# Rows of the expert tiles turned by DMA transposes of 2-byte halves and put together on VectorE, in place of transposes on TensorE

## The chip, the cores and the metric

The kernel runs on one core of a Trainium2 chip. The time is that of one execution on the device in microseconds, as a median over several executions. Before the change it is 495.23 us (three runs, 494.86 to 496.37). A run is called fast when it is undisturbed, and slow when it is over 1.5% above the fastest of its kernel. Each changed kernel was timed on the same chip and in the same rounds as the kernel before. A ratio is the mean time of one kernel's fast runs over the mean of the other's in the same rounds (for most experiments the first, profiled run is left out), so it isn't quite the ratio of the medians that stand beside it. The interval behind a ratio is at 95%. The experiments ran on several chips, where the kernel before had medians of 494.69 to 496.69 us. So a difference between the medians of two experiments is uncertain by some 2 us, and where it matters the difference of the ratios, times 495.5 us, stands beside it. A verdict "faster" or "slower" asks for 2%.

## The reference, cut to what matters

```python
def reference(q, k, v, lam, w_gate, w_local, w1, w2):
    x = linear_attention(q, k, v, lam)           # 4 x 768 tokens, 512 float32 each
    ... # pick one of 8 experts e[b, s] for each token (argmax of x @ w_gate, or the token before's)
    for b in range(B):
        for s in range(S):
            h = np.maximum(x[b, s] @ w1[e], 0.0)     # 512 x 1024
            out[b, s] = p[e] * (h @ w2[e])           # 1024 x 512
```

Attention comes first, then the experts. 3072 tokens are sorted by expert into tiles of 128 rows, with a few half tiles for the remainders. Everything is float32.

## The kernel before

Attention writes each token's row to a scratch tensor in DRAM. The expert part has 24 whole tiles and, with this input, three half tiles. For each tile, GpSimd gathers 128 rows with an indirect DMA. They arrive with tokens on the partitions, but the first product needs the 512 features there, so TensorE turns the tile in four 128x128 transposes and VectorE brings the result from PSUM to SBUF. SyncE issues the weight loads, 2 MB each for w1 and w2, two tiles ahead.

```python
    def rows_of(s):                                  # attention: rows to DRAM
        ...
        xn = moe.tile([P, DM], F32, name="xn")       # two buffers
        nc.scalar.copy(xn, px)
        nc.scalar.dma_start(out=x_dram[P * s:P * s + P, :], in_=xn)

    def weights(g):                                  # SyncE; skipped if the expert stays
        nc.sync.dma_start(out=w1t[g % 2], in_=w1_src(e), cond=other, cond_hint=False)
        nc.sync.dma_start(out=w2t[g % 2], in_=w2_src(e), cond=other, cond_hint=False)

    def ahead(g):                                    # gather, two tiles ahead
        collect(xgt[g % 2], *at(g))

    def turned(g):
        pt = pg.tile([P, DT, P], F32, name="po1")
        for d in range(DT):                          # DT = 4
            nc.tensor.transpose(pt[:, d], xgt[g % 2][:, P * d:P * d + P], ident)
        nc.vector.tensor_copy(xtt[g % 2], pt)

    # the stretch in which half tiles run between whole ones (three of eight steps)
            for g in range(GA, GB):
                ahead(g + 2)
                if g + 1 in half_in:
                    xh[half_in[g + 1]] = ahead_half(half_in[g + 1])
                hidden(g, 0)                         # first product
                if h is not None:
                    hs = hidden_of_half(xh.pop(h))
                hidden(g, 1)
                ...
                turned(g + 1)
                if g + 1 in half_in:
                    xh[half_in[g + 1]] = turned_half(xh[half_in[g + 1]])
                output(g)                            # second product
                ...
                weights(g + 2)
                if h is not None:
                    output_of_half(h, ht)
                    if h + 1 < n:
                        weights_of_half(h + 1)       # 4 MB more, for one half tile
```

## Time and profile before

| what | before |
|---|---|
| time, median | 495.23 us |
| TensorE busy | 475.2 us, 96% of the span |
| DMA share, 171 to 297 us (half tiles among the whole ones) | 1.01 |
| DMA share, 361 to 484 us | 0.50 |
| one whole tile late in the kernel | 14.45 us |

In all views PE is TensorE, PEld its weight loads, DVE VectorE, ACT ScalarE, POOL GpSimd and SP SyncE; L185 is a line of the kernel, and `out<-in` names the tiles written and read. The DMA share is the mean busy share of the 16 DMA engines.

Two things are read before anything else. Which engine is busy all the time? And what is second? The busy row of the page, its slices and the windows answer both, and the prediction shows them.

### The profile page before, as it was taken

How to read it: one execution, taken by the hardware profiler on the slowest of the kernel's cores; microseconds unless marked ns; L12 is line 12 of the kernel's file. 1: busy time of each engine (PE TensorE's matmuls, PEld its weight loads, DVE VectorE, ACT ScalarE, POOL GpSimd, SP SyncE). 2: the span in 40 equal slices, each digit the busy share in tenths (PEclk: the TensorE clock that was granted, in tenths of full speed). 3: DMA queues.
4: the chain of work that ended last, by engine and by line, in shares of the span. 5: the costliest groups of instructions: out<-in, count | busy, mean ns of one | idle time of the engine just before them, and what ended most of it. 6: DMA issues, size and time to landing. Idle time of an engine off the chain costs nothing. (4 is left out here: it accounts for less than half of the span.)

```text
span 493.0 us, 10193 instructions
## 1 busy us (share of the span) xinstructions
PE 475.2 (96%) x4231; PEld 351.6 (71%) x4231; DVE 127.3 (26%) x315; ACT 84.7 (17%) x212; POOL 106.8 (22%) x118
## 2 busy tenths in 40 slices
PE   6999999989999999999999999999999999999992
PEld 5877788776777667658657856876667777666770
DVE  6645677652367301011010101101110110110000
ACT  2256656331110000000000001000000000000000
POOL 5575564300101300221011100201101101110000
PEclk9899999999999999999999999999999999999997
DMA  7999999996788999999999997699954980894000
GB/s 272 411 418 380 352 342 330 401 368 233 260 319 292 324 378 399 395 376 397 398 333 386 398 398 277 211 330 319 327 194 157 310 314 31 284 332 169 23 25 17
DMA packets 49850, 146.42 MB, mean 297 GB/s; under 512 B 3244, under 2 KB 3244, under 8 KB 46960
## 3 DMA queue, kind: packets, MB, share of 16 engines
q1 hardware_dynamic: 42096, 125.86, 69.9%
q0 software_dynamic: 4224, 13.37, 7.1%
q10 hardware_dynamic: 3456, 6.29, 3.4%
q8 instruction: 36, 0.59, 0.5%
q14 instruction: 38, 0.31, 0.2%
HBM read 153.90 MB, written 12.98 MB: 338 GB/s over the span
## 5 line engine op out<-in xcount | busy, mean ns | idle before, releaser
L646 PEld LDWEIGHTS ps<-xt,w 128*128 128x128 f32 x1536 | 175.0, 192 | 14.0 <-issue 12.9
L646 PE MATMUL ps<-xt,w 128*128 128x128 f32 x1536 | 177.1, 276 | 0.8 <-DVE xt L631 0.8
L653 PE MATMUL pk<-w,ht 128*128 128x512 f32 x384 | 168.8, 592 | 0.0
L653 PEld LDWEIGHTS pk<-w,ht 128*128 128x128 f32 x384 | 71.1, 190 | 80.4 <-issue 80.4
L648 ACT ACTIVATE ht<-ps 128x512 f32<-128x512 f32 x48 | 28.7, 598 | 314.7 <-PE ps L646 314.2
L659 POOL DMA_INDIRECT out_dram<-y,sidx x24 | 24.6, 1026 | 196.3 <-DVE y L658 179.3
L658 DVE TENSOR_SCALAR y<-pk,gate 128x512 f32<-128x512 f32 x24 | 18.0, 751 | 146.0 <-PE pk L653 140.6
L637 DVE COPY xt<-po 128x512 f32<-128x512 f32 x23 | 15.9, 691 | 143.2 <-PE po L636 143.1
L621 POOL DMA_INDIRECT xg<-x_dram,gidx x24 | 25.0, 1041 | 121.2 <-PE po L636 84.1
L189 DVE TENSOR_TENSOR sm<-ps,mask 128x512 f32<-128x512 f32 x46 | 29.6, 685 | 15.1 <-PE ps L185 15.0
L165 POOL TENSOR_TENSOR qd<-inp,lamq 128x512 f32<-128x512 f32 x20 | 25.6, 1282 | 23.3 <-PE po L212 8.8
L185 PE MATMUL ps<-inp 64*64 64x128 f32 x736 | 26.3, 282 | 2.0 <-DMA inp<-in_qkv_dram 2.0
L225 PE MATMUL po<-sm,inp 128*64 128x128 f32 x384 | 26.9, 284 | 0.3 <-DMA inp<-in_qkv_dram 0.3
L225 PEld LDWEIGHTS po<-sm,inp 128*64 128x64 f32 x384 | 21.1, 140 | 7.5 <-issue 6.6
L168 POOL TENSOR_TENSOR kd<-inp,rev 128x512 f32<-128x512 f32 x20 | 22.4, 1122 | 16.1 <-PE pk L234 7.6
L185 PEld LDWEIGHTS ps<-inp 64*64 64x64 f32 x736 | 20.6, 136 | 5.6 <-issue 4.6
L246 ACT COPY xn<-pk 128x512 f32<-128x512 f32 x24 | 14.1, 588 | 30.6 <-DMA x_dram<-xn 19.8
L216 ACT ACTIVATE kv<-kv,lamq 128x64 f32<-128x64 f32 x64 | 17.1, 337 | 9.8 <-PE po L212 6.4
L228 ACT COPY xc<-po 128x256 f32<-128x256 f32 x48 | 15.3, 371 | 14.2 <-PE po L225 14.0
L244 PE MATMUL pk<-ident,xc 128*128 128x128 f32 x96 | 15.7, 286 | 0.0
L234 PE MATMUL pk<-inp,kd 128*64 128x64 f32 x320 | 13.2, 222 | 1.2 <-issue 1.1
L636 PE MATMUL po<-ident,xg 128*128 128x128 f32 x92 | 13.8, 273 | 0.0
(182 smaller groups left out, 223.6 us busy)
## 6 DMA issues: line engine op xcount, KB each, us to landing
w<-in_w_dram SPq DMA_DIRECT2D x57, 2048.0 KB
inp<-in_qkv_dram SPq DMA_DIRECT2D x22, 1024.0 KB
x_dram<-xn ACTq DMA_DIRECT2D x24, 256.0 KB
inp<-in_qkv_dram SPq DMA_DIRECT2D x4, 512.0 KB
w<-in_w_dram SPq DMA_DIRECT2D x4, 512.0 KB
xg<-x_dram,gidx POOLq DMA_INDIRECT x24, 7.0
out_dram<-y,sidx POOLq DMA_INDIRECT x24, 6.9
xgh<-x_dram,gidx POOLq DMA_INDIRECT x3, 6.4
```

The lines of the kernel that those rows point to most:

```text
L165: nc.gpsimd.tensor_tensor(qd, x[:, 0].rearrange("p (a i) -> p a i", i=P), lamq, ALU.mult)
L168: nc.gpsimd.tensor_tensor(kd.rearrange("p (h d) -> p h d", d=DH), x[:, 2].rearrange("p (h d) -> p h d", d=DH), rev.unsqueeze(2).broadcast_ ...
L185: nc.tensor.matmul(ps[u][js, a], lhsT=kt[rows, a, js], rhs=qt[rows, a], start=True, stop=True, skip_group_check=True)
L189: nc.vector.tensor_tensor(sm[:, u], ps[u], mask[:, u], ALU.mult)
L216: nc.scalar.mul(kv[:, a], kv[:, a], lamq[:, a, P - 1:P])
L225: nc.tensor.matmul(head(a, u), lhsT=vn[:, a, u], rhs=sm[:, u, a], start=(not c and a < 2), stop=True, skip_group_check=True)
L621: nc.gpsimd.indirect_dma_start(out=xg, out_offset=None, in_=x_dram[:n, :], in_offset=bass.IndirectOffsetOnAxis(ap=gidx[i][:, j:j + 1], axi ...
L646: nc.tensor.matmul(ph[:, i], lhsT=w1t[g % 2][:, d, P * f:P * f + P], rhs=xtt[g % 2][:, d], start=(d == 0), stop=(d == DT - 1))
L648: nc.scalar.activation(hts[g][:, FT // 2 * half:FT // 2 * half + FT // 2], ph, ACT.Relu)
L653: nc.tensor.matmul(pys[g % 2], lhsT=ht[:, f], rhs=w2t[g % 2][:, f], start=(f == 0), stop=(f == FT - 1))
L658: nc.vector.tensor_scalar(y, pys[g % 2], gate[i][:, j:j + 1], None, ALU.mult)
L659: nc.gpsimd.indirect_dma_start(out=out, out_offset=bass.IndirectOffsetOnAxis(ap=sidx[i][:, j:j + 1], axis=0), in_=y, in_offset=None, bound ...
```

## The change

The intent is to take the transposes off TensorE, which is the bound, and give them to the DMA engines. The DMA transpose is used here on 2-byte elements: a float32 row is stored as 512 low halves followed by 512 high halves. The tile of 128 x 1024 halves is transposed by DMA, SBUF to SBUF, and VectorE puts low and high halves together again. There is one hop more per tile, so there is a third row buffer, gathers start one tile earlier, and the transpose is issued by SyncE, in the queue of the weights. In attention, the row copy on ScalarE now splits the halves, and has four buffers in place of two.

```diff
+        xn = moe.tile([P, 2 * DM], U16, name="xn", bufs=4)
+        nc.scalar.copy(xn.rearrange("p (l f) -> p l f", l=2), px.bitcast(U16).rearrange("p (f l) -> p l f", l=2))
...
+    xgt = [moe.tile([P, 2 * DM], U16, name=f"xg{i}", bufs=1) for i in range(3)]
+    xct = [moe.tile([P, 2, DT, P], U16, name=f"xc{i}", bufs=1) for i in range(2)]
...
+    def cross(xc, xg):
+        nc.sync.dma_start_transpose(out=xc.rearrange("p l d i -> p (l d) i"), in_=xg)
...
     def turned(g):
-        pt = pg.tile([P, DT, P], F32, name="po1")
-        for d in range(DT):
-            nc.tensor.transpose(pt[:, d], xgt[g % 2][:, P * d:P * d + P], ident)
-        nc.vector.tensor_copy(xtt[g % 2], pt)
+        nc.vector.tensor_copy(xtt[g % 2].rearrange("p d i -> p (d i)").bitcast(U16).rearrange("p (k l) -> p l k", l=2),
+                              xct[g % 2].rearrange("p l d i -> p l (d i)"))
...
             for g in range(GA, GB):
                 h = half_in.get(g)
-                ahead(g + 2)
                 if g + 1 in half_in:
-                    xh[half_in[g + 1]] = ahead_half(half_in[g + 1])
+                    if half_in[g + 1] not in xh:
+                        xh[half_in[g + 1]] = ahead_half(half_in[g + 1])
+                    xh[half_in[g + 1]] = crossed_half(xh[half_in[g + 1]])
+                crossed(g + 2)
+                ahead(g + 3)
+                if g + 2 in half_in:
+                    xh[half_in[g + 2]] = ahead_half(half_in[g + 2])
                 hidden(g, 0)
... (the half tiles' copies and the other loops in the same way)
```

More of the change, by code (lines that the diff above doesn't have):

```diff
@@ L78 @@
     dram = ctx.enter_context(tc.tile_pool(name="dram", bufs=1, space=bass.MemoryType.DRAM))
-    x_dram = dram.tile([N, DM], F32, name="x_dram")
+    x_dram = dram.tile([N, 2 * DM], U16, name="x_dram")
     lt = route.tile([P, NT, E + 1], F32, name="lt")
@@ L244, in rows_of @@
             nc.tensor.transpose(px[:, P * a:P * a + P], xc[:, a, ORDER[s][0]], ident)
-        xn = moe.tile([P, DM], F32, name="xn")
-        nc.scalar.copy(xn, px)
+        xn = moe.tile([P, 2 * DM], U16, name="xn", bufs=4)
+        nc.scalar.copy(xn.rearrange("p (l f) -> p l f", l=2), px.bitcast(U16).rearrange("p (f l) -> p l f", l=2))
         nc.scalar.dma_start(out=x_dram[P * s:P * s + P, :], in_=xn)
@@ L612, in weights @@
         nc.sync.dma_start(out=w2t[g % 2], in_=w2_src(e), cond=other, cond_hint=False)
-    xgt = [moe.tile([P, DM], F32, name=f"xg{i}", bufs=1) for i in range(2)]
+    xgt = [moe.tile([P, 2 * DM], U16, name=f"xg{i}", bufs=1) for i in range(3)]
+    xct = [moe.tile([P, 2, DT, P], U16, name=f"xc{i}", bufs=1) for i in range(2)]
     xtt = [moe.tile([P, DT, P], F32, name=f"xt{i}", bufs=1) for i in range(2)]
@@ L623, in collect, with crossed, ahead_half @@
                                      bounds_check=n - 1, oob_is_err=False)
+    def cross(xc, xg):
+        nc.sync.dma_start_transpose(out=xc.rearrange("p l d i -> p (l d) i"), in_=xg)
     def ahead(g):
-        collect(xgt[g % 2], *at(g))
-    def first_turned():
-        for d in range(DT):
-            nc.tensor.transpose(pr[:, P * d:P * d + P], xgt[0][:, P * d:P * d + P], ident)
-        nc.vector.tensor_copy(xtt[0].rearrange("p d i -> p (d i)"), pr)
+        collect(xgt[g % 3], *at(g))
+    def crossed(g):
+        cross(xct[g % 2], xgt[g % 3])
+    def ahead_half(h):
+        xg = act.tile([P, 2 * DM], U16, name="xgh")
+        collect(xg, 1, GF - KA + h)
+        return xg
     def turned(g):
-        pt = pg.tile([P, DT, P], F32, name="po1")
-        for d in range(DT):
-            nc.tensor.transpose(pt[:, d], xgt[g % 2][:, P * d:P * d + P], ident)
-        nc.vector.tensor_copy(xtt[g % 2], pt)
+        nc.vector.tensor_copy(xtt[g % 2].rearrange("p d i -> p (d i)").bitcast(U16).rearrange("p (k l) -> p l k", l=2),
+                              xct[g % 2].rearrange("p l d i -> p l (d i)"))
     def hidden(g, half):
@@ L670 @@
         (18, 0): tokens_to_first_tiles, (19, 0): lambda: (brought(0, (0, 1)), masks(1)),
-        (19, 1): lambda: by_slots(0, (0, 1)), (20, 0): lambda: (ahead(0), ahead(1), rows_out(0)),
+        (19, 1): lambda: by_slots(0, (0, 1)), (20, 0): lambda: (ahead(0), ahead(1), ahead(2), rows_out(0)),
         (21, 0): lambda: chances(0), (22, 0): lambda: chances(1), (23, 0): lambda: brought(0, (2, 3, 4)),
+        (23, 1): lambda: turned(0),
     }
@@ L706 @@
                 nc.sync.dma_start(out=w2t[0], in_=w2_src(0))
-                nc.sync.dma_start(out=w1t[1], in_=w1_src(1))
-                nc.sync.dma_start(out=w2t[1], in_=w2_src(1))
-                weights(0)
-                weights(1)
             if s + 1 < NS:
@@ L721 @@
                 rows_of(s - 1)
-            if s + 1 == NS:
-                first_turned()
             if s % B == 0 and s:
@@ L726 @@
             extra_work(s, 1)
+            if s == NS - 4:
+                crossed(0)
+                crossed(1)
+                weights(0)
+                nc.sync.dma_start(out=w1t[1], in_=w1_src(1))
+                nc.sync.dma_start(out=w2t[1], in_=w2_src(1))
+                weights(1)
         x_ctx.close()
@@ L743 @@
         gates(NC - 1)
-        ahead(2)
+        crossed(2)
+        ahead(3)
         hidden(0, 1)
@@ L751 @@
         along_sequences(2)
-        ahead(3)
+        crossed(3)
+        ahead(4)
         hidden(1, 0)
@@ L762 @@
         tokens_to_other_tiles()
-        ahead(4)
+        crossed(4)
         hidden(2, 0)
@@ L776 @@
         ahead(6)
+        ahead(7)
+        first = ahead_half(0)
         rows_out(1)
@@ L779 @@
         hidden(4, 1)
+        crossed(5)
+        crossed(6)
         turned(5)
@@ L788, in weights_of_half, with crossed_half, turned_half @@
         nc.sync.dma_start(out=w2t[2], in_=w2_src(e))
-    def ahead_half(h):
-        xg = act.tile([P, DM], F32, name="xgh")
-        collect(xg, 1, GF - KA + h)
-        return xg
-    def turned_half(xg):
-        for d in range(DT):
-            nc.tensor.transpose(pr[:, P * d:P * d + P], xg[:, P * d:P * d + P], ident)
+    def crossed_half(xg):
+        xc = act.tile([P, 2, DT, P], U16, name="xch")
+        cross(xc, xg)
+        return xc
+    def turned_half(xc):
         xt = act.tile([P, DT, HP], F32, name="xth")
-        nc.vector.tensor_copy(xt, pr.rearrange("p (d i) -> p d i", i=P)[:, :, :HP])
+        nc.vector.tensor_copy(xt.rearrange("p d i -> p (d i)").bitcast(U16).rearrange("p (d i l) -> p l d i", l=2, i=HP),
+                              xc[:, :, :, :HP])
         return xt
@@ L841 @@
         weights(6)
-        first = ahead_half(0)
-        ahead(7)
+        first = crossed_half(first)
+        crossed(7)
+        ahead(8)
         hidden(5, 0)
@@ L887 @@
         for g in range(GB, GMIN - 1):
-            ahead(g + 2)
+            crossed(g + 2)
+            if g + 3 <= GMIN:
+                ahead(g + 3)
             hidden(g, 0)
@@ L898 @@
             for g in range(GMIN - 1, last):
-                if GMIN + 1 <= g + 2 < last:
-                    ahead(g + 2)
+                if GMIN < g + 2 < last:
+                    if g + 2 == GMIN + 1:
+                        ahead(g + 2)
+                    crossed(g + 2)
+                if GMIN < g + 3 < last:
+                    ahead(g + 3)
                 hidden(g, 0)
```

## The prediction

> **What bounds the kernel now.** I read the page's busy shares and slices first, then the costliest groups, then the timeline of TensorE in two places, then sums over windows, and last the queue that issues the weight loads.
>
> ```profile
> PE 475.2 (96%) x4231; PEld 351.6 (71%) x4231; DVE 127.3 (26%) x315; ACT 84.7 (17%) x212; POOL 106.8 (22%) x118
> ...
> PE   6999999989999999999999999999999999999992
> ...
> DMA  7999999996788999999999997699954980894000
> ```
>
> TensorE is busy in every slice but the first and the last; no other engine is near. But the DMA row stands at 9 in most slices up to the middle: two resources are close to full at once, and this change moves work from the first to the second.
>
> ```profile
> L646 PE MATMUL ps<-xt,w 128*128 128x128 f32 x1536 | 177.1, 276 | 0.8 <-DVE xt L631 0.8
> ...
> L637 DVE COPY xt<-po 128x512 f32<-128x512 f32 x23 | 15.9, 691 | 143.2 <-PE po L636 143.1
> ...
> L246 ACT COPY xn<-pk 128x512 f32<-128x512 f32 x24 | 14.1, 588 | 30.6 <-DMA x_dram<-xn 19.8
> ...
> L636 PE MATMUL po<-ident,xg 128*128 128x128 f32 x92 | 13.8, 273 | 0.0
> ```
>
> L636 are the transposes that go: 92, with 0.0 us of idle before them, 273 ns each by record. Records overlap, so their real price is read from starts:
>
> ```profile
> 426.64 7.31 PE L646 MATMUL ps<-xt,w 128*128 128x128 f32 x64
> 433.78 0.60 PE L636 MATMUL po<-ident,xg 128*128 128x128 f32 x4
> 434.22 7.03 PE L653 MATMUL pk<-w,ht 128*128 128x512 f32 x16
> 441.09 7.31 PE L646 MATMUL ps<-xt,w 128*128 128x128 f32 x64
> ```
>
> One tile is 441.09 - 426.64 = 14.45 us with no gap: first product 7.14, four transposes 434.22 - 433.78 = 0.44, second product 6.87. So a tile's transposes cost 0.44 us on the bound engine, not 0.60 and not 4 x 0.273. The first tile is different:
>
> ```profile
> 105.00 0.66 PE L244 MATMUL pk<-ident,xc 128*128 128x128 f32 x4
> 105.50 0.60 PE L630 MATMUL pr<-ident,xg 128*128 128x128 f32 x4
> 106.88 3.84 PE L646 MATMUL ps<-xt,w 128*128 128x128 f32 x32 [0.78 <-DVE xt L631]
> ```
>
> Here TensorE also waits 0.78 us for VectorE's copy. Now DMA, over the stretches of the expert part:
>
> ```profile
> 115.00:171.00 56.00, 55.91 (x339) 39.77 (x338) 28.12 (x87) 5.79 (x12) 8.56 (x8) 1.00 0.87 307
> 171.00:297.00 126.00, 126.00 (x756) 87.92 (x755) 13.36 (x29) 11.75 (x20) 19.38 (x19) 1.00 1.01 382
> 297.00:361.00 64.00, 64.00 (x392) 47.02 (x392) 6.26 (x9) 5.25 (x9) 9.19 (x9) 1.00 0.84 291
> 361.00:484.00 123.00, 123.00 (x695) 88.38 (x693) 11.55 (x16) 10.15 (x17) 14.25 (x14) 1.00 0.50 175
> ```
>
> The last two columns are DMA share and GB/s. From 171 to 297 us, where whole and half tiles both load weights, the 16 DMA engines are at 1.01 while TensorE is busy for all 126 us. The queue is already backed up:
>
> ```profile
> 177.41 4.54 SPq L611 DMA_DIRECT2D w<-in_w_dram  x1
> ```
>
> An issue that elsewhere takes 0.37 us took 4.54: it had to wait for room in the queue.
>
> **What the Trainium skill says.** (1) "DMA: Bandwidth & Descriptors", Latency and other measured facts: a DMA transpose reached 261 GB/s with a non-contiguous middle dimension, about 350-400 when contiguous. (2) "Advanced Engine Details and Errata", X-Bar Transpose (TRN2): transposes run about as fast as plain DMAs, but two transpose streams must not be in flight together; here all are issued by SyncE, so that is kept. (3) "VectorE: DVE Perf Modes", The three transpose paths: 1309 ns for 128x128 of 2 bytes by DMA against 390 on TensorE. The trace before has no DMA transpose, so it can't agree or disagree with these; for TensorE it shows 273 ns by record, and 0.11 us in a stream (0.44 / 4). (4) The same page, What auto-detection actually checks: a one-source operation with both sides in SBUF and even outer dimensions runs at two elements a cycle, whatever the stride. The old copy reads PSUM, so it is excluded, and its 691 ns for 512 elements in the trace fit one a cycle; the fast case isn't in this trace for 2-byte halves.
>
> **The change, part by part.**
>
> Removed from TensorE: 23 tiles x 0.44 = 10.1 us, all on the path; three half tiles at the same price (the timeline has the tile's transposes at 191.67, the half's at 192.10, the next product at 192.54), 3 x 0.44 = 1.3 us. At the first tile the transposes and the wait go, but VectorE is itself busy until about 105.4 us with the routing work ordered ahead of this copy; I let the first product start about 0.8 us earlier. Sum 12.2 us, or 2.5% of 495.2.
>
> Changed on VectorE: each 691 ns copy from PSUM becomes a copy of 1024 2-byte elements inside SBUF. At two a cycle that is again about 0.6 to 0.7 us by the skill's 0.96 GHz (512 cycles plus overhead), at one a cycle about 1.1 to 1.2 (estimates). VectorE has 13.4 us of work in 126, and the copy has the 6.87 us of the second product to hide in. Path: 0.
>
> Changed on ScalarE: the row copy handles 1024 elements for 512. This engine took 371 ns for 256 (L228) and 588 for 512, so 0.85 ns an element; estimate 588 + 512 x 0.85 = 1.02 us, or 24 x 0.43 = 10.4 us more in attention. ScalarE was busy 31.7 of 60 us from 46 to 106, so this fits. The four buffers take away its 19.8 us of waits for the row stores. TensorE there was busy 57.35 of 60 us and was not waiting for these copies. Path: 0 plus or minus 1 us.
>
> Added to DMA: one transpose of 128 x 1024 x 2 bytes = 256 KB per tile, 27 in all counting halves. Call its price, in time of all 16 engines, c. At 382 GB/s (what plain traffic reaches here) c = 0.69 us; at the skill's 261 GB/s c = 1.0 us; with something for the pieces' overhead and the end of each transpose I take 1.1 us. An unoverlapped eight times 1309 ns would be 10.5 us; I don't believe that for one instruction spread over 16 engines, but it marks the bad end.
>
> Moved: three row buffers let a gather (median 7.0 us to landing) start a tile earlier, which pays for the extra hop. The second expert's weights are now issued behind the first two transposes, near 100 us rather than 84; TensorE needs them at 124.4 us, and 4.2 MB take 11 us, so they arrive.
>
> Where DMA is full: from 171 to 297 us TensorE would now want to be done in 126 - 10 x 0.44 = 121.6 us, while DMA has 126 us of work and gets about 11 more transposes. The gap is 4.4 + 11c. Some of it is only a longer queue: a weight buffer is released at the end of one first product and read by the one after next, 22 to 30 us later, while its 2 MB take 5.5 us and those of two loads ahead 11. I estimate that about 12 us more backlog fits. So the stall is about 4.4 + 11c - 12, floor 0: 0.2 us at c = 0.69, 3.4 at 1.0, 4.5 at 1.1, 14 at 2.0. The three other stretches have room of 7, 10 and 61 us of DMA time and take 4 to 9 transposes each, so they stay with TensorE up to c near 1.7.
>
> Sum: 495.2 - 12.2 + 4.5 = 487.5 us.
>
> **The rivals.** *A: all of it is kept.* c is at most 0.7, or the backlog has more room than I estimate: 483 us. For it: TensorE never waited for a weight even at share 1.01. Against it: a share of 1.01 for 126 us, and the 4.54 us issue. *B: DMA becomes the bound.* c is 2 us or more, from small pieces or because a transpose drains its queue at its end: saving 12.2, stall 14, about 497 us; at c = 3 over 505 us. For it: the smaller the packets, the worse, and the skill's 1309 ns for an eighth of the size. Against it: its 350-400 GB/s. *C: order in the queue.* The transposes share SyncE's queue with the weights; SyncE waits for a gather before it issues one, and holds back the weights behind it; or a transpose waits behind 4 MB and arrives late. The load issued at 177.41 us is used at 199.4 and has three or four 2 MB loads ahead, so its room is a few us, and two transposes now go in before it. I expect 0 to 3 us there, inside the 4.5 us above. Elsewhere each transpose is issued more than a tile before its use. *D: ScalarE in attention.* A 1.02 us copy could hold up the copies that free the attention PSUM tile; 24 x 0.43 = 10.4 us if all of it were on the path, near 0 by its idle time.
>
> **Range and chances.** The certain part is 12.2 us on TensorE; the open part is c. 482 us needs A with a small gain in attention; 500 us is c a bit over 2. Two per cent is 9.9 us, 485.3 us, so over 2% faster needs a stall under 2.3 us, c under about 0.9: 0.37. Slower by over 2% (505 us) needs c near 3: 0.14. The rest, 0.49, is within 2%.
>
> **What would show it.** Right: TensorE's tile of 14.45 us becomes 14.0 late in the kernel, no L636 group is left, VectorE's copy is 0.6 to 0.7 us, ScalarE's row copy near 1.0 us, and any idle of TensorE in the expert part is put down to weight DMAs between 180 and 300 us, of about 4 us in sum. Wrong: TensorE waiting for the turned rows themselves (then the transpose's latency or its place in the queue is the matter, not bandwidth); SyncE's issues of transposes taking several us each; idle of TensorE spread over all tiles (c far over 2); or growth of the attention part before 105 us by over 1 us (rival D). If the tile shrinks by 0.44 and no stall shows, the backlog estimate was too small and the time is near 483.

## More of the kernel before

One line more, that of the SyncE queue on the page (packets, MB, share of the span of all 16 DMA engines), is kept for comparison, together with what TensorE waits for in the whole run (sum, times, longest):

```profile
q1 hardware_dynamic: 42096, 125.86, 69.9%
```

```profile
PE ps L185 <- DMA inp<-in_qkv_dram: 2.0, 1, 2.0
PE pk L683 <- POOL ident masks.py:199: 2.0, 1, 2.0
```

The largest waits are at the start and in attention. In the expert part there is none for weights.

## The result, and the profile after

The changed kernel takes 513.97 us (median of four runs, 509.93 to 517.67; one of them slow) against 495.49 of before in the same rounds. The ratio is 1.0344 (1.0268 to 1.0421): slower, by 3.4%, and outside the predicted range. The three fast runs alone have a median of 512.21 us; the differences below that start from 514.0 contain the slow run.

The page of the changed kernel, first its busy row, the slices of TensorE, its clock and DMA, and the DMA totals:

```profile
PE 471.0 (92%) x4123; PEld 343.7 (67%) x4123; DVE 128.3 (25%) x315; ACT 95.5 (19%) x212; POOL 109.5 (21%) x118
...
PE   6999899888999997899359998999999999999993
...
PEclk9899999998999999899869998999999999999997
DMA  7999899997999999999999999999899796599000
...
q1 hardware_dynamic: 70608, 132.94, 78.8%
```

TensorE has 108 instructions fewer, so the transposes are gone, but now it has holes: a 7, then a 3 and a 5 in the middle, where before were only nines. The DMA row is at 9 nearly to the end. SyncE's queue carried 7.1 MB more, but took 78.8% of 513.9 us instead of 69.9% of 493.0: 405.0 - 344.6 = 60.4 us of all 16 engines, or 2.24 us for each of the 27 transposes (so far an estimate: it puts all of the growth down to them).

The groups of the page (busy us, mean ns of one, idle before and what ended it) of the copies that the change altered, and of the half tile's first product:

```profile
L819 PE MATMUL pr<-w,xth 128*64 128x512 f32 x48 | 14.5, 759 | 18.1 <-DVE xth L811 18.1
...
L247 ACT COPY xn<-pk 128x1024 uint16<-128x1024 uint16 x24 | 24.3, 1014 | 18.2 <-PE pk L245 18.0
...
L642 DVE COPY xt<-xc 128x1024 uint16<-128x1024 uint16 x24 | 18.1, 754 | 21.4 <-DMA xc<-xg 21.2
...
L811 DVE COPY xth<-xch 128x512 uint16<-128x512 uint16 x3 | 1.4, 453 | 62.0 <-DMA xch<-xgh 62.0
```

The copies cost what was expected. The surprise is the first line: 18.1 us of idle TensorE in front of the half tiles, put down to VectorE's copy, which itself waited for the transpose (last line). VectorE is the messenger here, the DMA the cause.

The windows of the changed kernel, the middle and the end of the expert part (start and end, length, busy us and instructions of PE, PEld, DVE, ACT and POOL; then the TensorE clock that was granted, as a share of full speed, the DMA share and GB/s):

```profile
171.00:297.00 126.00, 106.38 (x593) 71.51 (x592) 12.07 (x26) 9.32 (x16) 17.89 (x18) 0.93 1.04 337
297.00:361.00 64.00, 61.92 (x365) 43.07 (x364) 6.55 (x10) 5.85 (x10) 8.36 (x8) 0.97 1.05 327
361.00:484.00 123.00, 123.00 (x714) 90.24 (x713) 13.01 (x18) 10.15 (x17) 18.22 (x16) 1.00 0.82 258
```

From 171 to 297 us TensorE is idle for 20 of 126 us, and the DMA engines, busier than before, move 337 GB/s in place of 382. They are occupied with something that isn't bytes. The timeline of TensorE, the lines of the expert part's middle that have a wait (start, duration, and in brackets the idle time and its releaser):

```profile
205.18 5.31 PE L652 MATMUL ps<-xt,w 128*128 128x128 f32 x32 [3.57 <-DMA w<-in_w_dram]
211.88 3.65 PE L819 MATMUL pr<-w,xth 128*64 128x512 f32 x16 [1.39 <-DVE xth L811]
262.65 5.47 PE L819 MATMUL pr<-w,xth 128*64 128x512 f32 x16 [14.66 <-DVE xth L811]
316.67 5.35 PE L819 MATMUL pr<-w,xth 128*64 128x512 f32 x16 [2.08 <-DVE xth L811]
```

Four waits make 21.7 us. The half tile's product after the longest wait takes 5.47 us, and after the shortest 3.65 for the same 16 matmuls. The clock granted in this stretch is 0.93, so a wait costs more than its own length. The trace's clock records have TensorE at half speed around each of these waits (204.9 to 208.3 us, 252.7 to 266.3 and 317.5 to 321.0), and once more behind a wait of 1.98 us for ScalarE (119.6 to 123.0). An experiment below, no_turn, has no such waits and no half speed between 90.5 and 479.6 us. TensorE worked for some 14 us of these pieces, which makes about 7 us lost (an estimate). Late in the kernel, where DMA has room, the saving is there as predicted:

```profile
476.87 7.31 PE L652 MATMUL ps<-xt,w 128*128 128x128 f32 x64
...
490.88 7.31 PE L652 MATMUL ps<-xt,w 128*128 128x128 f32 x64
```

490.88 - 476.87 = 14.01 us a tile, against 14.45. Last, SyncE's queue (start, duration of the issue), around the longest wait, and one transpose late in the kernel:

```profile
228.46 9.62 SPq L801 DMA_DIRECT2D w<-in_w_dram  x1
238.56 0.23 SPq L802 DMA_DIRECT2D w<-in_w_dram  x1
238.97 17.23 SPq L628 DMA_TRANSPOSE xch<-xgh  x1
...
443.93 1.29 SPq L628 DMA_TRANSPOSE xc<-xg  x1
```

The issue of 443.93 us, with no load or transpose in the queue, took 1.29 us. The half tile's transpose of 238.97 us took 17.23. As I read it, its pieces could only enter as room came free behind several loads of 2 MB. SyncE did nothing else meanwhile: its next issue started at 256.39 us. By the packet records its first piece moved at 256.08 and its last ended at 259.93 us. TensorE had stood since 247.99.

The packet records also show the shape of the new traffic. A transpose of 256 KB is 1024 packets of 256 bytes (and 32 of 4). The median packet takes 18 ns, but the mean over the kernel is 36.9 ns, with single packets of up to 3.4 us; all together 63.8 us of the 16 engines, 2.36 each. What stood in front of a transpose makes the difference. The 18 that came directly behind weights took 2.6 us of all engines in the mean (1.3 to 3.7). Of the six that came directly behind another transpose, three took 1.15 us, with 18.0 ns a packet and about 1.0 us of wall time, one 1.37, and two 2.7 and 3.2. Three found SyncE's queue idle and took 2.31, 2.25 and 1.39.

The records also show what the dear ones wait for. In 17 of the 18 behind weights, the long packets (over 150 ns, 9 to 23 in each transpose) end within 30 ns of one another, 0.26 to 0.38 us after the last packet of the weights in front. I read this so: engines that are through with their weights stand in the transpose until the last engine is through too. It need not be weights: the transpose of 3.2 us behind another, and the one of 2.25 on an idle queue, have 19 to 22 packets of 0.7 to 1.4 us that end together 0.8 us after a 16 KB packet of the instruction queue. For the one of 2.7 us I found no single reason; ScalarE's row stores ran beside it.

### The profile page after: what moved, and what is told of

Its sections match the earlier page's. It is cut to its first block, busy times and chain, and to the rows that moved or that the text cites. A ratio compares the mean times of both kernels' runs of the same rounds, so it can differ in the third digit from the quotient of the medians.

```text
span 513.9 us, 10012 instructions
## 1 busy us (share of the span) xinstructions
PE 471.0 (92%) x4123; PEld 343.7 (67%) x4123; DVE 128.3 (25%) x315; ACT 95.5 (19%) x212; POOL 109.5 (21%) x118
## 3 DMA queue, kind: packets, MB, share of 16 engines
q1 hardware_dynamic: 70608, 132.94, 78.8%
## 4 chain that ended last, share of the span: by engine, by line
DMA 27%; PE 16%; issue 8%; POOL 0%; DVE 0%; another core or an unknown queue 0%; SPq 0%; POOLq 0%; DVEq 0%
DMA xg<-x_dram,gidx 9%; DMA xch<-xgh 8%; PE pk L659 7%; PE ps L652 6%; DMA xc<-xg 6%; DMA out_dram<-y,sidx 4%; PE pr L819 2%; PE po L837 1%; POOL out_dram L665 0%; DVE xth L811 0%; PE pl L827 0%; SPq L613 0%; POOLq L665 0%; DVEq L642 0%
## 5 line engine op out<-in xcount | busy, mean ns | idle before, releaser
L665 POOL DMA_INDIRECT out_dram<-y,sidx x24 | 26.2, 1090 | 182.0 <-DVE y L664 143.4
L623 POOL DMA_INDIRECT xg<-x_dram,gidx x24 | 26.1, 1088 | 153.9 <-DMA xc<-xg 121.2
L190 DVE TENSOR_TENSOR sm<-ps,mask 128x512 f32<-128x512 f32 x46 | 29.6, 685 | 15.6 <-PE ps L186 15.4
L819 PE MATMUL pr<-w,xth 128*64 128x512 f32 x48 | 14.5, 759 | 18.1 <-DVE xth L811 18.1
L166 POOL TENSOR_TENSOR qd<-inp,lamq 128x512 f32<-128x512 f32 x20 | 25.6, 1282 | 22.2 <-issue 8.7
L247 ACT COPY xn<-pk 128x1024 uint16<-128x1024 uint16 x24 | 24.3, 1014 | 18.2 <-PE pk L245 18.0
L642 DVE COPY xt<-xc 128x1024 uint16<-128x1024 uint16 x24 | 18.1, 754 | 21.4 <-DMA xc<-xg 21.2
L819 PEld LDWEIGHTS pr<-w,xth 128*64 128x64 f32 x48 | 4.0, 173 | 26.5 <-DVE xth L811 18.7
L811 DVE COPY xth<-xch 128x512 uint16<-128x512 uint16 x3 | 1.4, 453 | 62.0 <-DMA xch<-xgh 62.0
```

The lines of the kernel that those rows point to most:

```text
L166: nc.gpsimd.tensor_tensor(qd, x[:, 0].rearrange("p (a i) -> p a i", i=P), lamq, ALU.mult)
L190: nc.vector.tensor_tensor(sm[:, u], ps[u], mask[:, u], ALU.mult)
L247: nc.scalar.copy(xn.rearrange("p (l f) -> p l f", l=2), px.bitcast(U16).rearrange("p (f l) -> p l f", l=2))
L623: nc.gpsimd.indirect_dma_start(out=xg, out_offset=None, in_=x_dram[:n, :], in_offset=bass.IndirectOffsetOnAxis(ap=gidx[i][:, j:j + 1], axi ...
L665: nc.gpsimd.indirect_dma_start(out=out, out_offset=bass.IndirectOffsetOnAxis(ap=sidx[i][:, j:j + 1], axis=0), in_=y, in_offset=None, bound ...
L819: nc.tensor.matmul(pr[HP * c:HP * c + HP], lhsT=xt[:, d], rhs=w1t[2][:, d, F // 2 * c:F // 2 * c + F // 2], start=(d == 0), stop=(d == DT ...
```

## The experiments

**The theory after reading.** (1) TensorE's saving of about 12 us is real. (2) A transpose behind weights costs twice what I took, because engines that are done with their share of the weights wait inside the transpose for the last one; this makes weights late. (3) The half tile's transposes stand in SyncE's order and in the queue behind weights and come late themselves. **Rivals.** All of the loss is bandwidth (then the order of the queue doesn't matter); all of it is order (then a plain copy in the same place costs as much); or the altered attention part is to blame.

Medians and ratios of all runs, with the kernel before's median of the same rounds:

| run | result | us | before | ratio (95%) |
|---|---|---|---|---|
| changed kernel | correct | 513.97 | 495.49 | 1.0344 (1.0268 to 1.0421) |
| no_turn | wrong | 483.39 | 494.69 | 0.9746 (0.9702 to 0.9791) |
| unread | wrong | 501.48 | 494.69 | 1.0158 (1.0106 to 1.0210) |
| plain_copy | wrong | 491.98 | 494.69 | 0.9940 (0.9914 to 0.9966) |
| half_on_pe | correct | 501.07 | 494.69 | 1.0107 (1.0072 to 1.0142) |
| act_queue | correct | 536.49 | 496.09 | 1.0805 (1.0732 to 1.0879) |
| unread_twice | wrong | 539.84 | 496.09 | 1.0854 (1.0779 to 1.0930) |
| four_buffers | correct | 493.58 | 496.09 | 0.9956 (0.9905 to 1.0007) |
| half_early | correct | 506.31 | 496.69 | 1.0189 (1.0120 to 1.0258) |
| act_ordered | correct | 514.65 | 496.69 | 1.0361 (1.0294 to 1.0428) |
| hybrid | correct | 493.44 | 496.69 | 0.9952 (0.9882 to 1.0022) |
| unread_in_threes | wrong | 499.08 | 496.03 | 1.0054 (1.0019 to 1.0090) |
| hybrid_earlier | correct | 489.31 | 496.03 | 0.9872 (0.9831 to 0.9912) |

### no_turn: the change without its transposes

VectorE reads the gathered rows as they are. The result is wrong; the work of all engines is otherwise that of the changed kernel.

```diff
     def cross(xc, xg):
-        nc.sync.dma_start_transpose(out=xc.rearrange("p l d i -> p (l d) i"), in_=xg)
+        pass
 ...
-                              xct[g % 2].rearrange("p l d i -> p l (d i)"))
+                              xgt[g % 3].rearrange("p (l k) -> p l k", l=2))
```

> The changed kernel without any DMA transpose: VectorE copies the gathered rows themselves, so the result is wrong on purpose; all other orders stay. Every theory puts the whole loss on the transposes' DMAs: TensorE is 11.4 us shorter than before and never waits in the expert part, so about 483 to 486 us (2 to 2.5% under before). If it is at 490 us or more, part of the loss lies elsewhere: in the attention part (the row copy, the four buffers, the later loads of the second expert), which was about 1.5 us late at the first product in the profiled run.

Measured: 483.39 us. Its window of the full stretch:

```profile
171.00:297.00 126.00, 125.86 (x741) 86.68 (x740) 13.54 (x27) 12.78 (x22) 20.71 (x20) 1.00 1.03 390
```

TensorE doesn't wait, at a DMA share of 1.03. So the whole saving on TensorE is there (about 12 us; 12.6 by the ratio of 0.9746), VectorE, ScalarE and the altered attention cost nothing that these runs resolve, and everything that the changed kernel loses, 514.0 - 483.4 = 30.6 us (29.6 by the ratios), comes with the transposes. The rival of the attention part falls.

### unread: the transposes run, but nobody waits for them

As no_turn, but `cross` is kept. What is left of the loss is the transposes' price on everybody else's transfers.

> The changed kernel with all 27 DMA transposes issued where they are, but nobody reads what they write: VectorE copies the gathered rows (wrong result on purpose). Theory Q (late arrival: the rows of the half tiles stand in SyncE's queue behind 4 to 6 MB of weights, and TensorE waits for them) expects the 18.1 us of waits at the half tiles and some 5 us of slower matmuls after the waits to go: 488 to 493 us. Theory B (bandwidth: 27 transposes take 60 us or so of all 16 DMA engines in a stretch that was full) expects the waits to move to the weights: 503 us or more.

Measured: 501.48 us. TensorE's waits in the full stretch:

```profile
198.69 6.49 PE L652 MATMUL ps<-xt,w 128*128 128x128 f32 x32 [4.56 <-DMA w<-in_w_dram]
294.30 6.47 PE L652 MATMUL ps<-xt,w 128*128 128x128 f32 x32 [6.59 <-DMA w<-in_w_dram]
```

They are now for weights. The time lies between what the two theories expected, nearer to that of bandwidth. The loss splits in two: 501.5 - 483.4 = 18.1 us (20.4 by the ratios), mostly because weights come late (one wait of 2.21 us, at 349.47 us, is for gathered rows), and 514.0 - 501.5 = 12.5 us (9.2 by the ratios) because the turned rows themselves come late.

### plain_copy: the same bytes at the same place, not turned

```diff
-        nc.sync.dma_start_transpose(out=xc.rearrange("p l d i -> p (l d) i"), in_=xg)
+        nc.sync.dma_start(out=xc.rearrange("p l d i -> p (l d i)"), in_=xg)
```

> Each DMA transpose replaced by a plain DMA copy of the same 256 KB, same queue, same place, same waits (rows of 2 KB instead of 1024 pieces of 256 B; wrong result on purpose). Theory Q says that the place in the queue is what counts, and the half tiles still wait: 500 us or more. Theory B with the small pieces as the cost (about 2.4 us of 16 engines' time for a transpose against 0.7 for a copy) says 486 to 490 us. A third theory S, that SyncE is held while it issues 1024 pieces into a full queue (issues of 5 to 17 us), also expects under 492 us, and issues of under 1 us.

Measured: 491.98 us. The profiled run, at 496.71 us, is the slowest of its five, so its waits are on the long side. TensorE's waits:

```profile
197.90 3.81 PE L652 MATMUL ps<-xt,w 128*128 128x128 f32 x32 [1.55 <-DMA w<-in_w_dram]
204.33 5.35 PE L819 MATMUL pr<-w,xth 128*64 128x512 f32 x16 [2.62 <-DVE xth L811]
246.59 6.51 PE L819 MATMUL pr<-w,xth 128*64 128x512 f32 x16 [4.45 <-DVE xth L811]
```

The same bytes in the same place of the queue cost 492.0 - 483.4 = 8.6 us (9.6 by the ratios), mostly late half rows: their bytes and their place already do harm without any turning. How much of it is the place alone wasn't tested. The turning costs the other 514.0 - 492.0 = 22.0 us (20.0). Neither "all order" nor "all bytes" stands, and none of the three expectations holds whole: theory S named this time, but also issues of under 1 us, and SyncE was held for up to 9.03 us by the issue of a plain copy. So being held isn't peculiar to transposes.

### half_on_pe: only the three half tiles back on TensorE

The half tile's rows aren't transposed by DMA; VectorE puts their halves together first, and TensorE turns them as before. The result is correct.

```diff
     def crossed_half(xg):
-        xc = act.tile([P, 2, DT, P], U16, name="xch")
-        cross(xc, xg)
-        return xc
+        return xg
     def turned_half(xc):
+        xw = act.tile([P, DM], F32, name="xwh", bufs=1)
+        nc.vector.tensor_copy(xw.bitcast(U16).rearrange("p (k l) -> p l k", l=2), xc.rearrange("p (l k) -> p l k", l=2))
+        for d in range(DT):
+            nc.tensor.transpose(pr[:, P * d:P * d + P], xw[:, P * d:P * d + P], ident)
```

> Only the three half tiles go back to TensorE (VectorE puts their halves together first, then four transposes and a copy); the 24 whole tiles keep the DMA transposes; the result is right. Theory Q expects the 18.1 us of waits and some 5 us of slower matmuls behind them to go for 1.3 us of transposes: 490 to 495 us. Theory B expects that three transposes of 27 matter little, since the other 24 still fill the DMA: 505 us or more.

Measured: 501.07 us, 12.9 less than the changed kernel (11.7 by the ratios), by taking away three of 27 transposes; the time lies between the two expectations. Two waits of the full stretch stay, 3.92 us for weights and 5.96 us in front of a half tile's turn, whose cause I didn't follow.

### half_early: the half tile's transpose ahead of the weights in SyncE's order

```diff
+        first = crossed_half(first)
         weights_of_half(0)
         weights(6)
-        first = crossed_half(first)
 ...
                     ht = hidden_turned(hs)
+                if g + 2 in half_in:
+                    xh[half_in[g + 2]] = crossed_half(xh[half_in[g + 2]])
                 turned(g + 1)
```

> The changed kernel with one edit of order: each half tile's DMA transpose is issued ahead of the weight loads that it stood behind (6 to 8 MB). Theory Q: the waits of TensorE for half rows (18.1 us and some 5 us of slower matmuls) go, and the late weights remain, as in the run with unread transposes: 499 to 504 us. If instead the time stays at 510 or more, the late rows were only the visible form of a full DMA and the wait moves to the weights.

Measured: 506.31 us, 7.7 less than the changed kernel and somewhat above what I expected. TensorE's larger waits:

```profile
205.09 6.46 PE L652 MATMUL ps<-xt,w 128*128 128x128 f32 x32 [5.89 <-DMA w<-in_w_dram]
249.46 3.65 PE L819 MATMUL pr<-w,xth 128*64 128x512 f32 x16 [1.86 <-DMA w<-in_w_dram]
303.67 6.66 PE L652 MATMUL ps<-xt,w 128*128 128x128 f32 x32 [7.65 <-DMA w<-in_w_dram]
```

No half tile waits for its rows any more. So the place in the order was the reason of that wait. But what stood behind the rows before now stands behind the transpose: the waits are for weights. By the ratios 7.7 of the 9.2 us for late rows come back, and what is left over unread (1.0189 against 1.0158) is within the noise.

### act_queue and act_ordered: the transposes out of the weights' queue

Both issue transposes from ScalarE. In act_queue all but the first two go there; in act_ordered those of tiles 0 to 6 stay on SyncE, the half tiles' and those from tile 7 on go to ScalarE, and ScalarE keeps the program's order in that part.

```diff
-        nc.sync.dma_start_transpose(out=xc.rearrange("p l d i -> p (l d) i"), in_=xg)
+        (by or nc.scalar).dma_start_transpose(out=xc.rearrange("p l d i -> p (l d) i"), in_=xg)
```

> The changed kernel with its DMA transposes issued by ScalarE (a queue of their own) instead of SyncE; only the first two stay on SyncE, before any of the others is in flight. Theory Q+R: (Q) in SyncE's queue they stand behind up to 8 MB of weights and hold SyncE; (R) behind weights a transpose takes 2.4 us instead of 1.0, because its packets wait until the last of the 16 DMA engines has finished its weights (packets of 18 ns that took up to 2275 ns). In a queue of its own every engine gets to it within a packet or so, so both go: waits for turned rows gone, about 1.1 us of DMA per transpose, 484 to 489 us. Theory B (256 KB in 256 B pieces simply cost 2.4 us of the DMA beside other traffic, whatever the queue) expects the late rows to go but not the late weights: 499 to 504 us, like the run with unread transposes.

> Transposes of tiles 0 to 6 on SyncE, all later ones from ScalarE, whose instructions now keep the program's order, so that one or two transposes and not four stand ahead of a ReLU. The run on ScalarE's queue before lost 47 us in three waits of TensorE for ScalarE (20.8, 14.9, 10.3), and had no other wait for weights or rows. Theory Q+R (place in the queue and waiting for the slowest DMA engine) expects those waits to go and 485 to 492 us, with packets of the transposes near 18 ns on the mean and each transpose about 10 us long beside weights. Theory B (the 2.4 us of DMA for each are inherent) expects late weights: 499 us or more.

Measured: 536.49 and 514.65 us. Both expectations missed. In act_queue:

```profile
197.64 9.01 PE L659 MATMUL pk<-w,ht 128*128 128x512 f32 x16 [20.83 <-ACT ht L654]
246.50 1.12 PE L827 MATMUL pl<-ident,hs 128*128 128x128 f32 x4 [14.91 <-ACT hs L822]
```

ScalarE was held by transposes as SyncE was, the one of the half tile among them:

```profile
177.36 12.93 ACTq L628 DMA_TRANSPOSE xch<-xgh  x1
```

Its next eviction (the copy of a product from PSUM to SBUF) started only at 196.99 us, and TensorE waited for that. In act_ordered that is mostly mended (12.1 us of such waits are left, of 46.9), and the largest wait is for weights again:

```profile
188.76 5.19 PE L659 MATMUL pk<-w,ht 128*128 128x512 f32 x8 [7.83 <-ACT ht L654]
...
307.47 5.62 PE L652 MATMUL ps<-xt,w 128*128 128x128 f32 x32 [10.64 <-DMA w<-in_w_dram]
```

Its full stretch has a DMA share of 1.03 at 341 GB/s, hardly more than the changed kernel's 337. That is the branch "late weights: 499 us or more" of theory B. The transposes' packets are short there, 21 to 23 ns in the mean, and in the full stretch each but the first took 8 to 14 us, as expected; but the weights' packets got longer: 98.5 ns for 2 KB against 91.2 in the kernel before, 175.0 for 4 KB against 164.2. By packet counts that is (7.3 x 9046 + 10.8 x 4121) / 16 = 6.9 us of all engines, and with the 15.3 us of the transposes' own packets 22.2 us for 10.7 transposes: about 2.1 us each (an estimate from these sums). The same sum for the changed kernel gives about 2.5. So a second queue moved most of the price into other packets and lowered it little.

### unread_twice: each transpose twice, neither read

```diff
+        nc.sync.dma_start_transpose(out=xcs.rearrange("p l d i -> p (l d) i"), in_=xg)
```

(added in the kernel of unread)

> The run with unread transposes, with each transpose issued twice in a row (the second into a scratch tile nobody reads; wrong result on purpose). Theory R (a wait for the slowest engine at each change from weights to a transpose, then 1.0 us) expects the second one to cost only about 1.0 us, as where two stood one behind the other: 11 in the full stretch, so 11 to 15 us over the run with single ones, 512 to 517 us. Theory B expects the full 2.4 us again for each: 26 us or more, 527 us or over.

Measured: 539.84 us; my expectation missed, and the time lies in the branch of theory B, 527 us or over. The 27 added transposes cost 38.4 us over unread, 1.42 us each (1.28 by the ratios). By their own packets 25 of them took 1.15 to 1.38 us of all engines and two 2.3 and 2.6, and the sum over all transposes' packets rose from 59.9 to 99.1 us, by 1.45 each. So the second of two is indeed cheaper than the first, but I had forgotten that one more us of DMA per tile makes the rest of the expert part DMA-bound too: the share from 361 to 484 us is 0.96 here. Both theories had left that out, and so this run alone doesn't tell them apart.

### unread_in_threes: the same 27 transposes, in fewer groups

The test that unread_twice should have been: the number stays, and only their neighbours change. In the full stretch three whole tiles' transposes and a waiting half tile's are issued directly behind one another every third step. Nobody reads them.

```diff
-                crossed(g + 2)
+                if g % 3 == 2 or n > 3:
+                    for xg in later:                 # half tiles put off until here
+                        crossed_half(xg)
+                    later.clear()
+                    for i in range(3) if g % 3 == 2 else ():
+                        crossed(g + i)
 ...
```

> Wrong on purpose, like the run in which nobody reads what the transposes turn (501.5 us, 18.1 us over the run without transposes). Here the same 27 transposes are issued, but those of the full stretch (steps 5 to 13) no longer one or two at a time before each tile's weights: three tiles' (and a half tile's) directly behind one another every third step, 3 groups in place of 9. Theory 'wait for the slowest engine': the dear part of a transpose is its first, behind weights (2.2 to 3.3 us of wall time); one directly behind another took 1.0 us. Six groups fewer at 1.2 us each give back about 7 us: 494 to 497 us, and more than half of the stretch's 256-byte packets lie in bursts at a mean of 18 ns. Rival 'each costs the same beside weights': 500 to 503 us as before. It would also be no gain, or a loss, if a burst of four transposes (4 us) in front of the weights cannot be made up by the weights' two buffers; then TensorE waits for weights right behind the bursts.

Measured: 499.08 us, ratio 1.0054 against unread's 1.0158, about 5.1 us less. That is outside the rival's range by the ratio, and short of the 7 us I expected. The packets of two of the groups, each transpose with the mean time of its packets and its time of all 16 engines (sums of the trace's packet records):

```
start     of      mean ns   us of 16 engines
254.03    half     47.0      3.01
256.90    whole    18.0      1.15
257.82    whole    21.3      1.36
259.67    whole    21.1      1.35
308.43    half     66.8      4.27
312.50    whole    18.0      1.15
313.42    whole    21.1      1.35
315.37    whole    21.1      1.35
```

The first of a group, which comes behind weights, takes 3.0 and 4.3 us; those behind it 1.15 to 1.36. Over the whole kernel, unread has 18 transposes directly behind weights at 2.6 us in the mean, this kernel 12 at 2.8; those directly behind another take 1.35 and 1.32. All transposes' packets took 54.9 us in place of unread's 59.9, and by the ratios the time fell by the same 5 us; the two intervals (1.0106 to 1.021 and 1.0019 to 1.009) don't meet. So the price of a transpose hangs on what stands in front of it. The two profiled executions don't show the gain in time: they took 498.7 and 498.9 us, and the waits for weights that stay, 4.44, 5.85 and 1.61 us, are in sum about those of unread.

### four_buffers: the kernel before with four row buffers

```diff
-        xn = moe.tile([P, DM], F32, name="xn")
+        xn = moe.tile([P, DM], F32, name="xn", bufs=4)
```

> The kernel before with only the second part of the change: four row buffers in attention instead of two. ScalarE's 19.8 us of waits for the row stores go. I expect no change of the end, within 0.3% of before (494 to 496 us), as TensorE didn't wait for these copies. A rival: the stores then come in bursts and delay the input loads, so attention is 1 to 2 us longer.

Measured: 493.58 us, ratio 0.9956 (0.9905 to 1.0007): no clear effect. ScalarE's 19.8 us of waits for the row stores weren't on the path that sets the end, and the buffers don't explain any of the loss.

### hybrid and hybrid_earlier: DMA transposes only where DMA has room

Tiles 5 to 13 and the half tiles, those of the full stretch, are turned on TensorE (after VectorE put their halves together); tiles 0 to 4 and 14 to 23 by DMA. Both give the correct result.

```diff
+ON_PE = range(5, 14)
     def crossed(g):
-        cross(xct[g % 2], xgt[g % 3])
+        if g not in ON_PE:
+            cross(xct[g % 2], xgt[g % 3])
 ...
```

> DMA transposes only where the DMA had room before: tiles 0 to 4 and 14 to 23 by DMA from SyncE, tiles 5 to 13 and the three half tiles on TensorE (VectorE puts the halves together first). Result right. If the loss comes only from transposes in the stretch where the DMA was full, TensorE doesn't wait there, 15 of 27 sets of transposes are saved: 483.4 + 12 x 0.44 = 488.7, say 487 to 491 us. If transposes hurt wherever weights are loaded, 493 us or more.

Measured: 493.44 us, above what I expected and in the branch "transposes hurt wherever weights are loaded". But the trace has another reason: all weights are in time, and each half tile's turn waited for VectorE:

```profile
190.85 0.66 PE L821 MATMUL pr<-ident,xwh 128*128 128x128 f32 x4 [1.43 <-DVE xwh L819]
```

There are three such waits of 1.43 us: the joining of the half tile's rows stood in VectorE's order behind the whole tile's copy. hybrid_earlier does both joinings between the two parts of the first product:

```diff
                 hidden(g, 0)
                 ...
+                if g + 1 in ON_PE:
+                    early_xw[g + 1] = joined(g + 1)
+                if g + 1 in half_in:
+                    xh[half_in[g + 1]] = joined_half(xh[half_in[g + 1]])
                 hidden(g, 1)
```

> Correct result. The mixed kernel (tiles 0 to 4 and 14 to 23 by DMA, 5 to 13 and the half tiles on TensorE) ran 493.4 us, with three waits of 1.43 us of TensorE for VectorE's putting together of a half tile's rows, which stood in VectorE's order behind the whole tile's. Here VectorE puts both together before the second half of the tile's hidden layer. Theory: those 4.3 us and nothing else come back: 488 to 490.5 us, faster than before by 1.0 to 1.5%, and no wait of TensorE over 0.5 us in steps 5 to 13. Rival: VectorE, now with two more copies of 0.75 us ahead of nothing it evicts, delays something else, or the DMA engines do; then 492 to 495 us, and the waits show for what.

Measured: 489.31 us, ratio 0.9872 (0.9831 to 0.9912). Its window of the full stretch:

```profile
171.00:297.00 126.00, 126.00 (x755) 87.92 (x755) 19.76 (x34) 11.71 (x20) 20.86 (x20) 1.00 1.02 388
```

TensorE is busy for all of the 126 us again. The 4.3 us came back (493.44 - 489.31 = 4.1). This version is faster than the kernel before by 1.3%, clear of the noise, and than the changed one by 4.6% (by the ratios). It is what is left of the change where it pays. Of the 483.4 us of no_turn it lacks the 12 tiles and half tiles that stay on TensorE, 12 x 0.44 = 5.3 us, which nearly closes the sum: 488.7.

## Why the prediction was wrong

It said 487.5 us, 482 to 500, with a chance of 0.14 for slower by over 2%. It is 514.0. Its own steps in their order:

- **TensorE saves 12.2 us: right.** A late tile takes 14.01 us instead of 14.45, and no_turn has 483.4 us, what the prediction named for "all of it is kept". The 0.8 us for an earlier first product isn't shown: in the profiled runs with the altered attention it starts between 104.4 and 108.4 us, against 106.88 before.
- **VectorE 0.6 to 0.7 us, ScalarE 1.02 us, no cost on the path: right.** They took 754 and 1014 ns, and no_turn contains both. The first is a little over the estimate and hidden all the same. At one element a cycle of the 0.96 GHz that the page gives, 1024 elements would take 1.07 us (an estimate), so the trace agrees with two a cycle for the strided copy inside SBUF, as the Trainium skill states it in "VectorE: DVE Perf Modes", What auto-detection actually checks.
- **The four buffers: right that ScalarE's waits didn't matter.** They gain nothing that the runs resolve.
- **c = 1.1 us per transpose: wrong, and the first step that failed.** This is a term of the sum that was mis-sized. By the queue's share it was 2.24 us. The 1.1 us that I took does exist, for a transpose directly behind another (1.15 at best). Behind weights, which is where this kernel puts 18 of 27, it is 2.6 in the mean. I had computed c from a rate, bytes over GB/s, and a transpose in a mixed queue has a price for the change from one kind to the other. The packet records fit this reading: single packets take up to 3.4 us, and behind weights they end together right after the last weights packet in front (17 of 18). So the wait for the last engine is read from the trace, and unread_in_threes shows that fewer such changes cost less; no run takes the wait alone away.
- **The stall 4.4 + 11c - 12: the form was right.** With c = 2.2 it gives 16.6 us; unread lost 18.1 us (20.4 by the ratios), mostly to late weights. (Its 0.2 us at c = 0.69 should be 0.0; nothing rests on that.) The prediction's table of c ends at "14 at 2.0" and rival B at "c = 3 over 505 us", so the mechanism was on the page, with too low a chance.
- **"The three other stretches … stay with TensorE up to c near 1.7": hardly tested.** c was above that; from 297 to 361 us the share rose to 1.05, but the one wait of 2.08 us there was for half rows. From 361 us on, with 61 us of room, TensorE lost nothing.
- **Rival C, "I expect 0 to 3 us there": wrong, and the second step that failed.** It was 12.5 us (the changed kernel less unread; 9.2 by the ratios). The supporting sentence, "elsewhere each transpose is issued more than a tile before its use", is false for the half tiles: in the diff, `crossed_half` for the half tile of step g + 1 stands at the start of step g, behind the weights of the step before. Also, I looked at how long SyncE waits *before* it issues a transpose, and not at how long the issue itself takes when the queue is full: up to 17.23 us, during which no weight load is issued either. The slow issue of 177.41 us in the profile before was the hint; I took it as a sign of bandwidth, not of an engine that is held.
- **Rival D, attention: right that it is near 0.** no_turn has the altered attention and keeps the whole saving.

The sum with the measured terms: 495.5 - 12.2 + 18.1 + 12.5 = 513.9 us. That it closes proves little, since the two losses are differences of the same runs; by the ratios it is 495.5 - 12.6 + 20.4 + 9.2 = 512.5, the mean of the fast runs. The two losses aren't independent: half_early, which takes away only the late rows, got 7.7 us back, and its waits are for weights. So 12.5 us is what late rows cost on top of late weights, not what mending them would give.

The prediction's list of what would show it wrong held: TensorE waiting for turned rows and issues of several us are both in the profile. What I should have done with it is ask for each of them, in the diff, how many loads stand ahead at that moment.

## What to carry to other kernels

Work moved from a full engine to a full queue isn't free because it is few bytes: ask what each new transfer stands behind, what stands behind it, and which engine is held while it is issued. Use DMA transposes where the DMA share has room and leave the others where they were (489.3 us here against 514.0), and if they must go beside large loads, issue several in a row (here this gave 5 of 18 us, in a kernel whose result is wrong; no correct kernel with it was timed). When two expectations share a blind spot, as in unread_twice, change neighbours or order and keep the count, so that only the disputed thing moves.

## What the Trainium skill lacked or had wrong

- "DMA: Bandwidth & Descriptors", Latency and other measured facts: its 261 GB/s for a DMA transpose holds here only for one directly behind another (256 KB in about 1.0 us). Directly behind weight loads the same transpose took 2.6 us of all 16 engines in the mean. The page doesn't say that the neighbours matter, nor that pieces of a transpose wait until the last engine is through with what stands in front (in 17 of 18 the long packets end together, 0.26 to 0.38 us after it).
- "Advanced Engine Details and Errata", X-Bar Transpose (TRN2): that transposes are as fast as regular DMAs isn't so in this mixed queue: 513.97 us with them (ratio 1.0344), 491.98 us (0.994) with plain copies of the same bytes in the same places.
- No page says how long the issue of a DMA transpose holds its engine when loads stand ahead. "DMA: Bandwidth & Descriptors" has a transpose's sequencer cycles only in a table about trn3 and earlier chips, without the transfer. Here SyncE was held 1.29 us with nothing in the queue and up to 17.23 us behind loads; on ScalarE transposes in the engine's order left TensorE waiting 20.83 us for an eviction.
